# A gated scan and MLP kernel on one core: range guards of five units checked at the end, no clip of slopes, one running sum over three parts

## The chip, the cores and the metric

The kernel runs on one core of a Trainium2 chip. The metric is the device time of one execution in microseconds. Three timed executions of the kernel before took 581.10, 581.84 and 581.97 us, median 581.84 us. The engines named here are TensorE (PE, with its weight loads as PEld), VectorE (DVE), ScalarE (ACT), GpSimd (POOL) and SyncE (SP, which here only issues DMAs).

## The reference

A complex decay is applied to a state per head, step by step, and its output goes through a two-layer MLP with a quadratic-linear activation.

```
# q, k, v, a_re, a_im: [4, 8, 768, 48] f32; a_re and a_im are drawn 8 times as large
mag = sqrt(a_re**2 + a_im**2)
scale = minimum(mag, 0.999) / (mag + 1e-6)
ar, ai = a_re * scale, a_im * scale
for t in range(768):                       # S_re, S_im: [4, 8, 48, 48]
    S_re, S_im = ar*S_re - ai*S_im + k[t] (x) v[t], ar*S_im + ai*S_re
    y[t] = q[t] . S_re
x = y as 3072 rows of 384
h = x @ w_in                               # 384 -> 2048
g = where(h >= 1, h, where(h <= -1, 0, (h + 1)**2 / 4))
out = g @ w_out                            # 2048 -> 384
```

## The kernel before

**Units and blocks.** The 4 x 768 tokens are 12 units of 256 tokens: three parts of each of four sequences, in the order of `BATCH` and `PART`. Two units make a block of 512 tokens, so there are six blocks. A unit passes through `gates(u)`, which turns the step-by-step decay into closed form, and `attend(u)`, which computes its attention on PE. `moe(blk)` then runs the MLP of a block: 16 steps, each of 9 matmuls of 512 columns into `h` (line 1128) and 9 into `o` (line 1203), with ACT and DVE computing `g` and its split in two parts between them.

**What `gates` does.** `AI` holds the real part A and the imaginary part I of the decay, 128 x 768 values each (three parts `j` of 256 tokens). A Relu of A whose sum goes to a guard table `fsum` (a READ_ACCUMULATOR follows each such instruction), Ln and Exp of A for its reciprocal, the product I/A on DVE (the slope, line 589), a clip of the slope to +-1.5 (line 592), Square of the slope, a second Square with a sum of fourth powers for the guard, Ln, a combination on DVE (601), Exp, and a second combination (611) give the log decay. All these ACT instructions are recorded under one line, 576. Then come the running sum of the log decay over time, Exp of it both ways, the product with k and q (690), Arctan of the slope, a running sum of the angles, its reduction by whole turns, two Sins, and two products (799). The results `x` and `kq` are spread by DMA into the head layout `hd`, from which `attend` reads.

Units 0 and 1 hold tokens on partitions, and their running sums are matmuls with a triangle of ones on PE (630). In units 2 to 11 each running sum is three scans of 256 elements on DVE, one for each part j (lines 671 and 721), which start from the last column of the part before. The scans of the decay use min with a cap of 40.

**What else competes.** 16 weight tiles are decoded (`weights`): a load (`raw_i`, `raw_o`), three to four DVE operations of 128 x 768 (lines 440, 449, 458, 469), a cast on ACT (464), for the first five of them two matmul groups on PE (478, 479). They share DVE and ACT with the gates. In the last block `ranges(k)` loads all 16 weight tiles once more (`chk`) and runs two accumulating ACT instructions on each (lines 513, 521). Both bear on whether the fast path's assumptions hold: at the end all guard sums are compared with bounds, a flag is formed on PE and DVE, and only if one fails does `scan_all`, a slow path, run.

**What sets the order.** Every operation is noted in a `Plan` with a cost, its inputs and outputs, and for some PE work and DMAs a due time. `Plan.order` passes due times backwards, then simulates the engines and always takes the ready operation that is due first; an operation without a due time comes when nothing else is ready, unless a more urgent one is about to be (`HOLD`). The program is emitted in that order, and each engine executes its own instructions strictly in it. `Plan.emit` also fills gaps that the plan expects on PE with idle matmuls (line 1256) to keep its clock up. `tl(turn_of("g", 4), ...)` hands out four buffers in turn to `AI`, `X` and `KQ` of the units and, after them, to `chk`; a load into one waits until all who used it before are done. `ranges` also waits for the last block's inputs and for the outputs of the earlier blocks (`after=`). ACT loads a function table before each group of Ln/Exp or of Arctan/Sin (`table`); Abs, Relu, Square and Copy need none.

Of the kernel before, what the change touches and what calls it, by code (L numbers as in the profile page):

```python
# [10 lines left out]
F32 = mybir.dt.float32  # L11
F32R = mybir.dt.float32r
U32 = mybir.dt.uint32
I32 = mybir.dt.int32
AF = mybir.ActivationFunctionType
ALU = mybir.AluOpType
AX = mybir.AxisListType

P = 128
# [8 lines left out]
NJ = DM // P  # L28
NF = DFF // P
CH = 128  # L30
HC = CH // 2
U = 256
# [8 lines left out]
PLACE = [b * NPART + p for b, p in zip(BATCH, PART)]  # L41
# [3 lines left out]
SLOT = {h: i for i, h in enumerate(sum(GROUPS, ()))}  # L45

SUM = 1.0e6
RATIO = 1.5
FOURTH = 1.142**4
TINY = 1e-18  # L50
DECAY = 40.0
T_MIN = 2.0**-15 * (1.0 + 2.0**-8)
# [8 lines left out]
DMA_FIX, DMA_END, DMA_ISSUE, LANES = 2400, 50, 470, 8  # L61
LOAD, MOVE = 410.0, 240.0
# [13 lines left out]
LEAD = 9000  # L76
WARM = 0.75
ABS_ACT = 5
LO_PE = 5
INFLATE = 1.6  # L80
SPLIT_DUE = 3000
# [203 lines left out]
def dve(n, two=False):  # L285
    return 66 + n / (1.92 if two else 0.96)


def act(n, ptr=False, acc=False, psum=False):
    return (80 if psum else 100) + (92 if ptr else 0) + (92 if acc else 0) + n * (0.77 if psum else 0.84)  # L290
# [25 lines left out]
def gated_scan_moe(  # L316
    ctx: ExitStack, tc: tile.TileContext, kq, ari, art, v, wl, qn, kn, arn, ain, vn, out
):
    nc = tc.nc

    const = ctx.enter_context(tc.tile_pool(name="const", bufs=1))
# [22 lines left out]
    held = [const.tile([P, 4, CH], F32, name=f"am{g}") for g in range(2)]  # L344
    for t in held:
        nc.gpsimd.memset(t, 0.0)
    consts = [math.log(1e-6), math.pi / 2, 0.5, TINY, T_MIN, 0.0, 1.0, DECAY]
    cst = const.tile([P, len(consts)], F32, name="cst")
    for i, c in enumerate(consts):
        nc.gpsimd.memset(cst[:, i : i + 1], c)  # L350
    c_eps, c_pi2, c_half, c_tiny, c_tin, zero, c_one, c_top = (
        cst[:, i : i + 1] for i in range(len(consts))
    )
    ones = c_one
# [4 lines left out]
    minus = const.tile([P, P], F32R, name="minus")  # L359
    nc.scalar.mul(minus, ident, -1.0)  # L360
    fsum = const.tile([P, 2, NU], F32, name="fsum")
    wsum = const.tile([P, 2, NF], F32, name="wsum")
    fdec = const.tile([P, NB, NJ], F32, name="fdec")
    state = const.tile([P, 2, 2, NJ], F32, name="state")

    pl = Plan()
# [14 lines left out]
    def tl(slot, shape, dtype, name, space=None):  # L381
        if slot in banks:
            return pl.tile(slot, lambda: view(banks[slot], shape))
        return pl.tile(
            slot, lambda: (space or sb).tile(shape, dtype, tag=slot, name=name, bufs=1)
        )
# [12 lines left out]
    def turn_of(tag, n):  # L399
        k = seen.get(tag, 0)  # L400
        seen[tag] = k + 1
        return f"{tag}{k % n}"

    V_, A_, PE_ = nc.vector, nc.scalar, nc.tensor
# [126 lines left out]

    heads, vt = {}, {}
    moved = []

    def gates(u):
# [32 lines left out]
        def ac(out, src, f, r, w, tab=False, **kw):  # L570
            acc_ = kw.get("accum_out")
            cost = act(N, ptr=not isinstance(kw.get("bias", 0.0), float), acc=acc_ is not None)
            pl.op(
                "ACT",
                cost,
                lambda: A_.activation(out(), src(), f, **kw),  # L576
                r=[*r] + ([TAB] if tab else []),
                w=w,
            )

        def ve(cost, fn, r, w):
            return pl.op("DVE", cost, fn, r=r, w=w)

        ac(A, A, AF.Relu, [a], [a], accum_out=acc(0))
        if u > 1:
            table("natural_log_exp_and_others")
        ac(X0, A, AF.Ln, [a], [x0], True, bias=c_tiny)
        ac(A, X0, AF.Exp, [x0], [a], True, scale=-1.0)
        ve(dve(N), lambda: V_.tensor_tensor(I(), I(), A(), op=ALU.mult), [a], [i])
        ve(  # L590
            dve(N, True),
            lambda: V_.tensor_scalar(I(), I(), RATIO, -RATIO, op0=ALU.min, op1=ALU.max),
            [],
            [i],
        )
        ac(A, I, AF.Square, [i], [a])
        ac(X1, A, AF.Square, [a], [x1], accum_out=acc(1))
        ac(A, A, AF.Ln, [], [a], True, bias=c_one)
        ve(
            dve(N),  # L600
# [4 lines left out]
            [x0],  # L605
        )
        ac(X1, X0, AF.Exp, [x0], [x1], True, bias=c_eps)
        SUMS, sums_ = (A, a) if by_token else (X0, x0)
        ve(
            dve(N),  # L610
            lambda: V_.scalar_tensor_tensor(
                SUMS(), X0(), -math.log(0.999), X1(), op0=ALU.max, op1=ALU.add
            ),
            [x0, x1],
            [sums_],
        )
        js = ((0, 2), (2, 3))

        def running(src, part_, slots, name):
# [21 lines left out]
                out.append(R)  # L641
            return out

        if by_token:
            D_ = running(A, a, ("o0", "o1"), "dec")
            for (j0, j1), R in zip(js, D_):
                ve(
                    80,
                    lambda j0=j0, j1=j1, R=R: V_.tensor_copy(
                        state[:, b % 2, 0, j0:j1], R.get()[:, :, U - 1]  # L650
                    ),
                    [R],
                    [(STATE[0], j0)],
                )
            for e, sign in ((1, -1.0), (0, 1.0)):
                for (j0, j1), R in zip(js, D_):
                    pl.op(
                        "ACT",
                        act((j1 - j0) * U, psum=True),
                        lambda j0=j0, j1=j1, R=R, e=e, sign=sign: A_.activation(  # L660
                            X.get()[:, j0:j1, e], R.get(), AF.Exp, scale=sign
                        ),
                        r=[R, TAB],
                        w=[(X, e)],
                    )
        else:
            for j in range(NJ):
                prev = state[:, b % 2, 0, j : j + 1] if part else 0.0
                i_ = ve(
                    100 + U / 0.48,  # L670
                    lambda j=j, prev=prev: V_.tensor_tensor_scan(
                        X0()[:, j],
                        X0()[:, j],
                        c_top.to_broadcast([P, U]),
                        prev,
                        op0=ALU.add,
                        op1=ALU.min,
                    ),
                    [STATE[0]] if part else [],
                    [x0],  # L680
                )
                if j:
                    pl.loose.add(i_)
            dst = fdec[:, b] if last else state[:, b % 2, 0]
            ve(80, lambda: V_.tensor_copy(dst, X0()[:, :, U - 1]), [x0], [STATE[0]])
            ac(X1, X0, AF.Exp, [x0], [x1], True, scale=-1.0)
            ac(X0, X0, AF.Exp, [], [x0], True)

        dma(2 * size, lambda: KQ.get(), lambda: kq[place], w=[KQ], after=moved if u == 2 else ())
        ve(dve(2 * N), lambda: V_.tensor_tensor(KQ.get(), KQ.get(), X.get(), op=ALU.mult), [X], [KQ])  # L690
# [6 lines left out]
        if by_token:  # L697
            for (j0, j1), R in zip(js, running(I, i, TOKEN[u], "turns")):
                ints = lambda j0=j0, j1=j1: I()[:, j0:j1].bitcast(I32)
                ve(  # L700
                    dve((j1 - j0) * U),
                    lambda ints=ints, R=R: V_.tensor_scalar(
                        ints(), R.get(), c, None, op0=ALU.mult
                    ),
                    [R],
                    [i],
                )
                ve(
                    dve((j1 - j0) * U),
                    lambda ints=ints, R=R, j0=j0, j1=j1: V_.scalar_tensor_tensor(  # L710
                        A()[:, j0:j1], R.get(), c, ints(), op0=ALU.mult, op1=ALU.subtract
                    ),
                    [R, i],
                    [a],
                )
        else:
            for j in range(NJ):
                prev = state[:, b % 2, 1, j : j + 1] if part else 0.0
                i_ = ve(
                    100 + U / 0.48,  # L720
                    lambda j=j, prev=prev: V_.tensor_tensor_scan(
                        A()[:, j],
                        I()[:, j],
                        zero.to_broadcast([P, U]),
                        prev,
                        op0=ALU.add,
                        op1=ALU.add,
                    ),
                    [i] + ([STATE[1]] if part else []),
                    [a],  # L730
                )
                if j:
                    pl.loose.add(i_)
            ve(
                dve(N, True),
                lambda: V_.tensor_scalar(I().bitcast(I32), A(), c, None, op0=ALU.mult),
                [a],
                [i],
            )
            ve(  # L740
                dve(N),
                lambda: V_.scalar_tensor_tensor(
                    A(), A(), c, I().bitcast(I32), op0=ALU.mult, op1=ALU.subtract
                ),
                [i],
                [a],
            )
# [529 lines left out]
    for blk in range(NBLK):  # L1277
        for u in BLOCKS[blk]:
            if u > 2:
                list(gates(u))  # L1280
            if u > 1:
                attend(u)
        if blk == NBLK - 1:
            for k in range(NF):
                ranges(k)
        moe(blk)
# [264 lines left out]
```

## Time and profile before

| what | value |
| --- | --- |
| median of three timed executions | 581.84 us |
| the profiled execution's own time | 582.15 us |
| its span, first to last instruction | 580.4 us |
| mean granted PE clock | 0.988 |
| busy PE / PEld / DVE / ACT | 559.4 / 465.1 / 443.1 / 388.3 us |
| first MLP matmul starts | 75.64 us |
| last MLP matmuls end | 572.99 us |

The profiled execution took 1.75 us more than its span, which lies before the first and after the last instruction. Busy time counts idle matmuls too (24.1 us in the group of line 1256), so the 96% of PE does not mean that the whole span is useful work. "idle before <-releaser" in a line is the time for which the engine stood still before that instruction, and what ended it. An ACT or DVE instruction may start a little before the end of the one ahead of it, so what one costs on a full engine is the distance from its start to the next start.

### The profile page before, as it was taken

The page shows a single profiled execution, that of the slowest core. Times are in us where ns is not written, and L with a number is a line of the kernel's source. Part 1 is how long each engine was busy: PE and PEld are TensorE (multiplying, and loading weights), DVE is VectorE, ACT ScalarE, POOL GpSimd, SP SyncE. Part 2 cuts the span into 40 slices and gives each one's busy share as a digit, 9 for nine tenths or more (in the row PEclk, how much of TensorE's full clock was granted, in tenths as well). Part 3 has the DMA queues.
Part 4 walks back from the last instruction along what each step waited for, and adds up shares of the span by engine and source line. Part 5 has one row for each costly group of instructions (what it writes and reads, how often), then busy time and mean ns, then how long its engine had stood idle before and what let it go on. Part 6 is the DMA issues. An engine that isn't in the chain of part 4 may idle for free.

```text
span 580.4 us, 10668 instructions
## 1 busy us (share of the span) xinstructions
PE 559.4 (96%) x4250; PEld 465.1 (80%) x4250; DVE 443.1 (76%) x641; ACT 388.3 (67%) x626; POOL 3.3 (1%) x24
## 2 busy tenths in 40 slices
PE   7899789999999999999999999999999999999994
PEld 6778768888888888888888888888888888888883
DVE  6898899989979979888996787896864545454443
ACT  8886779988986766677757556667433333369972
POOL 2000000000000000000000000000000000000000
PEclk9799899999999999999999999999999999999998
DMA  8838363574460531623502513402412200087721
GB/s 348 319 115 249 135 187 148 153 238 153 152 200 19 158 110 30 215 76 97 171 1 77 190 55 101 165 3 59 152 55 84 75 1 8 13 306 256 262 88 60
DMA packets 22953, 76.66 MB, mean 132 GB/s; under 512 B 4464, under 2 KB 10224, under 8 KB 22896
## 3 DMA queue, kind: packets, MB, share of 16 engines
q1 hardware_dynamic: 22896, 75.91, 39.4%
q8 instruction: 35, 0.57, 0.4%
q14 instruction: 22, 0.18, 0.1%
HBM read 51.12 MB, written 4.72 MB: 96 GB/s over the span
## 4 chain that ended last, share of the span: by engine, by line
PE 86%; DVE 5%; DMA 3%; ACT 2%; issue 1%; SPq 1%; DVEq 0%; ACTq 0%
PE o L1203 34%; PE h L1128 34%; PE at L955 5%; PE at L999 3%; PE at L1007 3%; PE at L924 3%; PE at L895 2%; DMA hd<-kq 1%; DMA raw_i<-in_wl_dram 1%; ACT ai L576 1%; SPq L411 1%; PE o L630 1%; ACT x L576 1%; DVE kq L799 1%; DVE x L799 1%
## 5 line engine op out<-in xcount | busy, mean ns | idle before, releaser
L1128 PE MATMUL h<-xH,wi 128*128 128x512 f32 x576 | 180.9, 395 | 1.0 <-ACT xH L1098 0.8
L1203 PE MATMUL o<-gh,wo 128*128 128x512 f32 x576 | 180.0, 394 | 0.0
L1128 PEld LDWEIGHTS h<-xH,wi 128*128 128x128 f32 x576 | 105.8, 188 | 23.9 <-ACT xH L1098 1.0
L1203 PEld LDWEIGHTS o<-gh,wo 128*128 128x128 f32 x576 | 106.4, 188 | 22.3 <-issue 0.3
L1128 PE MATMUL h<-xL,wi 128*128 128x512 f32 x288 | 112.6, 391 | 0.2 <-DVE xL L1105 0.2
L1203 PE MATMUL o<-gl,wo 128*128 128x512 f32 x288 | 112.3, 390 | 0.0
L1172 DVE TENSOR_TENSOR g<-h,s 128x512 f32<-128x512 f32 x96 | 65.9, 686 | 56.2 <-ACT s L1153 48.9
L1186 ACT CAST gh<-g 128x512 fp32r<-128x512 f32 x96 | 59.3, 617 | 55.8 <-DVE g L1180 52.1
L1153 ACT ACTIVATE s<-h,cst 128x512 f32<-128x512 f32 x96 | 65.5, 684 | 42.5 <-PE h L1128 37.7
L1190 DVE TENSOR_TENSOR gl<-g,gh 128x512 fp32r<-128x512 f32 x96 | 66.0, 687 | 32.6 <-ACT gh L1186 32.3
L1128 PEld LDWEIGHTS h<-xL,wi 128*128 128x128 f32 x288 | 54.1, 188 | 12.2 <-DVE xL L1105 0.6
L1203 PEld LDWEIGHTS o<-gl,wo 128*128 128x128 f32 x288 | 54.1, 188 | 11.5
L576 ACT ACTIVATE ai<-ai 128x768 f32<-128x768 f32 x53 | 44.5, 844 | 25.6 <-DMA ai<-in_ari_dram 7.9
L1180 DVE SCALAR_TENSOR_TENSOR g<-s,g 128x512 f32<-128x512 f32 x80 | 55.3, 691 | 2.3
L955 PEld LDWEIGHTS at<-hd 96*64 96x64 f32 x704 | 32.6, 137 | 9.9 <-issue 8.2
L955 PE MATMUL at<-hd 96*64 96x128 f32 (+1 forms) x704 | 37.1, 251 | 1.8 <-DMA hd<-kq 1.8
L967 DVE COPY_PREDICATED am<-tri,at 128x512 f32<-128x512 uint32 x44 | 31.6, 738 | 2.5 <-PE at L955 2.4
L1007 PE MATMUL at<-am,V 128*64 128x128 f32 x352 | 32.9, 273 | 0.0
L999 PE MATMUL at<-hd,st 96*64 96x128 f32 x304 | 30.5, 278 | 0.0
L420 ACT ACT_TABLE_LOAD x21 | 26.9, 1283 | 0.3
L1256 PE MATMUL idle<-tri,ident 128*128 128x128 f32 x170 | 24.1, 301 | 1.8 <-POOL tri masks.py:66 1.8
L1256 PEld LDWEIGHTS idle<-tri,ident 128*128 128x128 f32 x170 | 23.2, 215 | 2.6 <-POOL tri masks.py:66 1.8
(119 smaller groups left out, 653.3 us busy)
## 6 DMA issues: line engine op xcount, KB each, us to landing
chk<-in_wl_dram SPq DMA_DIRECT2D x16, 768.0 KB, 6.5
kq<-in_kq_dram SPq DMA_DIRECT2D x12, 768.0 KB, 5.7
ai<-in_ari_dram SPq DMA_DIRECT2D x10, 768.0 KB, 6.9
V<-in_v_dram SPq DMA_DIRECT2D x12, 576.0 KB, 4.1
hd<-x SPq DMA_DIRECT2D x24, 288.0 KB, 3.5
hd<-kq SPq DMA_DIRECT2D x24, 288.0 KB, 4.1
raw_i<-in_wl_dram SPq DMA_DIRECT2D x8, 768.0 KB, 8.3
raw_o<-in_wl_dram SPq DMA_DIRECT2D x8, 768.0 KB, 4.5
```

Of the source, the lines that this page charges most:

```text
L576: lambda: A_.activation(out(), src(), f, **kw),
L955: PE_.matmul(SC.get()[o : o + HC, i + e, HC * k :], t[:, 0, ks], t[:, 1, qs], start=True, stop=True,)
L999: PE_.matmul(o_, st.get().rearrange("p h e -> p (h e)")[:, lo : lo + 64], head(h)[:, 1, cs], start=True, stop=False,)
L1007: PE_.matmul(o_, V.get()[:, c, lo : lo + 64], ams[pr // 2].get()[:, 2 * (pr % 2) + e, :], start=st is None, stop=True,)
L1128: PE_.matmul(H.get(), weight["i", f // 2].get()[:, f % 2, part, sl], x.get()[:, j, :], start=j == 0 and n == 0, stop=j == NJ - 1 and n == 2,)
L1153: lambda: A_.activation(SS.get(), H.get(), AF.Relu, bias=c_half, scale=-0.5 if spare else 0.5),
L1172: lambda: V_.tensor_tensor(G.get(), H.get(), SS.get(), op=ALU.max),
L1180: lambda: V_.scalar_tensor_tensor(G.get(), SS.get(), 1.0, G.get(), op0=ALU.min, op1=ALU.mult),
L1186: pl.op("ACT", act(T), lambda: A_.copy(GH.get(), G.get()), r=[G], w=[GH])
L1190: lambda: V_.tensor_tensor(GL.get(), G.get(), GH.get().bitcast(F32), op=ALU.subtract),
L1203: PE_.matmul(PO[m].get(), weight["o", f // 2].get()[:, f % 2, part, sl], g.get(), start=f == 0 and n == 0, stop=f == NF - 1 and n == 2,)
L1256: PE_.matmul(idle["h1"], ident, mask, start=True, stop=True)
```

## The change

Five things change in `gates`, and one function is new.

1. For units 0 to 4 (`LATE = 5`) the Relu with its sum and the second Square with its sum are left out of `gates`. The values that follow do not use their outputs as long as A is not negative.
2. For all 12 units the clip of the slope is left out.
3. For units 2 to 11 the three scans of each running sum become one scan of 768 elements (`total`). A row `again` of unsigned bytes, 0 at each part's first token and 1 elsewhere, multiplies the running value, which resets it. In parts after a sequence's first, the state of the part before is added to the first column of each part by a DVE operation of its own. The cap of 40 in the scan goes; the bound on the last value is still compared at the end.
4. The log decay is written to A instead of X0 in units 2 to 11, and the two Exps read it there.
5. `slopes(u)` reloads `AI` of units 0 to 4 and checks them: two accumulating Relus and one accumulating Abs on ACT, one DVE operation between, in which 1.142 A - |I| is formed. It is noted in the plan ahead of `ranges`, with no due time and no `after=`.

```diff
@@ -11,6 +11,7 @@
 F32 = mybir.dt.float32
 F32R = mybir.dt.float32r
 U32 = mybir.dt.uint32
+U8 = mybir.dt.uint8
 I32 = mybir.dt.int32
 AF = mybir.ActivationFunctionType
 ALU = mybir.AluOpType
@@ -45,8 +46,8 @@
 SLOT = {h: i for i, h in enumerate(sum(GROUPS, ()))}
 
 SUM = 1.0e6
-RATIO = 1.5
-FOURTH = 1.142**4
+SLOPE = 1.142
+FOURTH = SLOPE**4
 TINY = 1e-18
 DECAY = 40.0
 T_MIN = 2.0**-15 * (1.0 + 2.0**-8)
@@ -76,6 +77,7 @@
 LEAD = 9000
 WARM = 0.75
 ABS_ACT = 5
+LATE = 5
 LO_PE = 5
 INFLATE = 1.6
 SPLIT_DUE = 3000
@@ -344,11 +346,11 @@
     held = [const.tile([P, 4, CH], F32, name=f"am{g}") for g in range(2)]
     for t in held:
         nc.gpsimd.memset(t, 0.0)
-    consts = [math.log(1e-6), math.pi / 2, 0.5, TINY, T_MIN, 0.0, 1.0, DECAY]
+    consts = [math.log(1e-6), math.pi / 2, 0.5, TINY, T_MIN, 1.0]
     cst = const.tile([P, len(consts)], F32, name="cst")
     for i, c in enumerate(consts):
         nc.gpsimd.memset(cst[:, i : i + 1], c)
-    c_eps, c_pi2, c_half, c_tiny, c_tin, zero, c_one, c_top = (
+    c_eps, c_pi2, c_half, c_tiny, c_tin, c_one = (
         cst[:, i : i + 1] for i in range(len(consts))
     )
     ones = c_one
@@ -359,7 +361,12 @@
     minus = const.tile([P, P], F32R, name="minus")
     nc.scalar.mul(minus, ident, -1.0)
     fsum = const.tile([P, 2, NU], F32, name="fsum")
-    wsum = const.tile([P, 2, NF], F32, name="wsum")
+    nc.gpsimd.memset(fsum[:, 1, :LATE], 0.0)
+    wsum = const.tile([P, 2, NF + LATE], F32, name="wsum")
+    again = const.tile([P, NJ * U], U8, name="again")
+    nc.gpsimd.memset(again, 1.0)
+    for j in range(NJ):
+        nc.gpsimd.memset(again[:, j * U : j * U + 1], 0.0)
     fdec = const.tile([P, NB, NJ], F32, name="fdec")
     state = const.tile([P, 2, 2, NJ], F32, name="state")
 
@@ -530,6 +537,47 @@
         )
 
 
+
+    def slopes(u):
+        AI = tl(turn_of("g", 4), [P, 2, NJ, U], F32, f"far_{u}")
+        A, I = (lambda: AI.get()[:, 0]), (lambda: AI.get()[:, 1])
+        N = NJ * U
+        pl.op(
+            "SP",
+            DMA_ISSUE,
+            lambda: nc.sync.dma_start(AI.get(), ari[PLACE[u]]),
+            w=[AI],
+            dma=2 * P * N * 4 / LOAD,
+        )
+        pl.op(
+            "ACT",
+            act(N, acc=True),
+            lambda: A_.activation(I(), I(), AF.Abs, accum_out=wsum[:, 0, NF + u : NF + u + 1]),
+            w=[(AI, 1)],
+        )
+        pl.op(
+            "DVE",
+            dve(N),
+            lambda: V_.scalar_tensor_tensor(
+                I(), A(), SLOPE, I(), op0=ALU.mult, op1=ALU.subtract
+            ),
+            r=[(AI, 0)],
+            w=[(AI, 1)],
+        )
+        pl.op(
+            "ACT",
+            act(N, acc=True),
+            lambda: A_.activation(A(), A(), AF.Relu, accum_out=fsum[:, 0, u : u + 1]),
+            w=[(AI, 0)],
+        )
+        pl.op(
+            "ACT",
+            act(N, acc=True),
+            lambda: A_.activation(
+                I(), I(), AF.Relu, scale=-1.0, accum_out=wsum[:, 1, NF + u : NF + u + 1]
+            ),
+            w=[(AI, 1)],
+        )
 
     heads, vt = {}, {}
     moved = []
@@ -581,20 +629,16 @@
         def ve(cost, fn, r, w):
             return pl.op("DVE", cost, fn, r=r, w=w)
 
-        ac(A, A, AF.Relu, [a], [a], accum_out=acc(0))
+        if u >= LATE:
+            ac(A, A, AF.Relu, [a], [a], accum_out=acc(0))
         if u > 1:
             table("natural_log_exp_and_others")
         ac(X0, A, AF.Ln, [a], [x0], True, bias=c_tiny)
         ac(A, X0, AF.Exp, [x0], [a], True, scale=-1.0)
         ve(dve(N), lambda: V_.tensor_tensor(I(), I(), A(), op=ALU.mult), [a], [i])
-        ve(
-            dve(N, True),
-            lambda: V_.tensor_scalar(I(), I(), RATIO, -RATIO, op0=ALU.min, op1=ALU.max),
-            [],
-            [i],
-        )
         ac(A, I, AF.Square, [i], [a])
-        ac(X1, A, AF.Square, [a], [x1], accum_out=acc(1))
+        if u >= LATE:
+            ac(X1, A, AF.Square, [a], [x1], accum_out=acc(1))
         ac(A, A, AF.Ln, [], [a], True, bias=c_one)
         ve(
             dve(N),
@@ -605,14 +649,13 @@
             [x0],
         )
         ac(X1, X0, AF.Exp, [x0], [x1], True, bias=c_eps)
-        SUMS, sums_ = (A, a) if by_token else (X0, x0)
         ve(
             dve(N),
             lambda: V_.scalar_tensor_tensor(
-                SUMS(), X0(), -math.log(0.999), X1(), op0=ALU.max, op1=ALU.add
+                A(), X0(), -math.log(0.999), X1(), op0=ALU.max, op1=ALU.add
             ),
             [x0, x1],
-            [sums_],
+            [a],
         )
         js = ((0, 2), (2, 3))
 
@@ -641,6 +684,30 @@
                 out.append(R)
             return out
 
+        def total(dst, src, q, own, w):
+            if part:
+                ve(
+                    80,
+                    lambda: V_.tensor_tensor(
+                        src()[:, :, 0], src()[:, :, 0], state[:, b % 2, q], op=ALU.add
+                    ),
+                    [STATE[q]],
+                    [own],
+                )
+            ve(
+                100 + N / 0.48,
+                lambda: V_.tensor_tensor_scan(
+                    dst().rearrange("p j t -> p (j t)"),
+                    again,
+                    src().rearrange("p j t -> p (j t)"),
+                    0.0,
+                    op0=ALU.mult,
+                    op1=ALU.add,
+                ),
+                [own] if own is not w else [],
+                [w],
+            )
+
         if by_token:
             D_ = running(A, a, ("o0", "o1"), "dec")
             for (j0, j1), R in zip(js, D_):
@@ -664,27 +731,11 @@
                         w=[(X, e)],
                     )
         else:
-            for j in range(NJ):
-                prev = state[:, b % 2, 0, j : j + 1] if part else 0.0
-                i_ = ve(
-                    100 + U / 0.48,
-                    lambda j=j, prev=prev: V_.tensor_tensor_scan(
-                        X0()[:, j],
-                        X0()[:, j],
-                        c_top.to_broadcast([P, U]),
-                        prev,
-                        op0=ALU.add,
-                        op1=ALU.min,
-                    ),
-                    [STATE[0]] if part else [],
-                    [x0],
-                )
-                if j:
-                    pl.loose.add(i_)
+            total(A, A, 0, a, a)
             dst = fdec[:, b] if last else state[:, b % 2, 0]
-            ve(80, lambda: V_.tensor_copy(dst, X0()[:, :, U - 1]), [x0], [STATE[0]])
-            ac(X1, X0, AF.Exp, [x0], [x1], True, scale=-1.0)
-            ac(X0, X0, AF.Exp, [], [x0], True)
+            ve(80, lambda: V_.tensor_copy(dst, A()[:, :, U - 1]), [a], [STATE[0]])
+            ac(X1, A, AF.Exp, [a], [x1], True, scale=-1.0)
+            ac(X0, A, AF.Exp, [a], [x0], True)
 
         dma(2 * size, lambda: KQ.get(), lambda: kq[place], w=[KQ], after=moved if u == 2 else ())
         ve(dve(2 * N), lambda: V_.tensor_tensor(KQ.get(), KQ.get(), X.get(), op=ALU.mult), [X], [KQ])
@@ -714,23 +765,7 @@
                     [a],
                 )
         else:
-            for j in range(NJ):
-                prev = state[:, b % 2, 1, j : j + 1] if part else 0.0
-                i_ = ve(
-                    100 + U / 0.48,
-                    lambda j=j, prev=prev: V_.tensor_tensor_scan(
-                        A()[:, j],
-                        I()[:, j],
-                        zero.to_broadcast([P, U]),
-                        prev,
-                        op0=ALU.add,
-                        op1=ALU.add,
-                    ),
-                    [i] + ([STATE[1]] if part else []),
-                    [a],
-                )
-                if j:
-                    pl.loose.add(i_)
+            total(A, I, 1, i, a)
             ve(
                 dve(N, True),
                 lambda: V_.tensor_scalar(I().bitcast(I32), A(), c, None, op0=ALU.mult),
@@ -1281,6 +1316,8 @@
             if u > 1:
                 attend(u)
         if blk == NBLK - 1:
+            for u in range(LATE):
+                slopes(u)
             for k in range(NF):
                 ranges(k)
         moe(blk)
```

## The prediction

> **What bounds the kernel now.** I read the page's 40 slices first, then the busy time by stretch, and then, since the answer pointed to the first 85 us, the timelines of ACT, DVE and PE there.
>
> From the page, the busy tenths of PE and ACT:
>
> ```profile
> PE   7899789999999999999999999999999999999994
> ACT  8886779988986766677757556667433333369972
> ```
>
> From the busy time by stretch (columns: length; busy us of PE, PEld, DVE, ACT, POOL; granted clock; DMA share; GB/s):
>
> ```profile
> 0.00:16.00 16.00, 10.56 (x60) 9.29 (x60) 10.98 (x17) 13.15 (x21) 3.28 (x24) 0.93 0.88 355
> 16.00:45.00 29.00, 27.43 (x144) 21.66 (x146) 26.95 (x37) 23.65 (x38) 0.00 (x0) 0.92 0.58 199
> 45.00:61.00 16.00, 12.66 (x239) 11.72 (x238) 13.84 (x20) 10.74 (x18) 0.00 (x0) 1.00 0.89 292
> 61.00:76.00 15.00, 13.73 (x194) 13.01 (x194) 14.10 (x18) 10.90 (x18) 0.00 (x0) 0.89 0.25 78
> 76.00:85.00 9.00, 7.00 (x51) 5.03 (x50) 7.78 (x13) 8.31 (x15) 0.00 (x0) 1.00 0.60 168
> 85.00:260.00 175.00, 174.88 (x1400) 144.92 (x1399) 156.88 (x225) 136.62 (x212) 0.00 (x0) 1.00 0.43 140
> 260.00:425.00 165.00, 165.00 (x1292) 137.27 (x1289) 137.44 (x198) 104.71 (x161) 0.00 (x0) 1.00 0.31 96
> 425.00:510.00 85.00, 85.00 (x605) 70.35 (x604) 40.78 (x62) 30.07 (x52) 0.00 (x0) 1.00 0.15 44
> 510.00:567.00 57.00, 57.00 (x253) 47.18 (x252) 30.25 (x44) 46.78 (x94) 0.00 (x0) 1.00 0.63 226
> ```
>
> From 85 us to the last MLP matmul PE is busy without a break (174.88 of 175, 165 of 165, 85 of 85, 57 of 57) at full clock. The change takes no matmul away. So behind 85 us nothing taken from ACT or DVE is worth time, and the end moves by as much as the start of that unbroken stretch moves. Ahead of it PE is only filled with idle matmuls; the stretch is a chain of units 0, 1 and 2 through ACT, DVE and DMA, with the weight decode as filler. That is the stage in which the change has to pay. A change of this kernel below about 0.2% (1.16 us) can't be told from none.
>
> **The change part by part: the guards of units 0 and 1.** This is ACT's timeline of the start (start, length, instruction); rows that carry no term are left out:
>
> ```profile
> 4.04 0.84 ACT L576 ACTIVATE ai<-ai 128x768 f32<-128x768 f32 x1 [2.01 <-DMA ai<-in_art_dram]
> ...
> 4.88 0.29 ACT L360 ACTIVATE minus<-ident 128x128 fp32r<-128x128 f32 x1
> 5.08 0.93 ACT L576 ACTIVATE x<-ai,cst 128x768 f32<-128x768 f32 x1
> 5.94 0.84 ACT L576 ACTIVATE ai<-ai 128x768 f32<-128x768 f32 x1
> ...
> 6.78 0.83 ACT L576 ACTIVATE ai<-x 128x768 f32<-128x768 f32 x1
> ...
> 9.22 0.84 ACT L576 ACTIVATE ai<-ai 128x768 f32<-128x768 f32 x1
> 10.10 0.84 ACT L576 ACTIVATE x<-ai 128x768 f32<-128x768 f32 x1
> ...
> 10.94 0.83 ACT L576 ACTIVATE ai<-ai 128x768 f32<-128x768 f32 x1
> ...
> 12.50 0.83 ACT L576 ACTIVATE x<-ai 128x768 f32<-128x768 f32 x1
> ...
> 13.46 0.94 ACT L576 ACTIVATE ai<-ai,cst 128x768 f32<-128x768 f32 x1
> 14.30 0.92 ACT L576 ACTIVATE x<-x,cst 128x768 f32<-128x768 f32 x1
> ...
> 16.75 0.83 ACT L576 ACTIVATE ai<-ai 128x768 f32<-128x768 f32 x1
> ...
> 19.50 0.60 ACT L660 ACTIVATE x<-o 128x512 f32<-128x512 f32 x1 [1.47 <-PE o L630]
> ...
> 25.00 1.28 ACT L420 ACT_TABLE_LOAD   x1
> ```
>
> ACT stands still until unit 0's A lands, and then no row has a wait in brackets until 19.50: for 13 us ACT is the limit. Four of these instructions go: the Relus of units 0 (4.04) and 1 (5.94), each with its read of the sum, and their second Squares (10.10 and 12.50). On a full engine each costs the distance to the next start: 4.04 to 4.88, 5.94 to 6.78 and 10.10 to 10.94 are 0.84 us each, 12.50 to 13.46 is 0.96. That is 3.48 us, 3.36 if I count the last like the others. I take 3.4.
>
> Does something else take ACT's place? DVE's rows and the first running sums on PE:
>
> ```profile
> 7.64 0.96 DVE L589 TENSOR_TENSOR ai<-ai 128x768 f32<-128x768 f32 x1 [3.52 <-ACT ai L576]
> 8.63 0.56 DVE L592 TENSOR_SCALAR ai<-ai 128x768 f32<-128x768 f32 x1
> 15.47 0.95 DVE L611 SCALAR_TENSOR_TENSOR ai<-x 128x768 f32<-128x768 f32 x1
> 16.57 4.15 PE L630 MATMUL o<-tri,ai 128*128 128x256 f32 x12
> 21.41 2.12 PE L630 MATMUL o<-tri,ai 128*128 128x256 f32 x12
> ```
>
> DVE waits 3.52 us for ACT, so it is not late at first. Unit 0's chain alone, without any queue: the first Exp would start one Relu earlier at 5.94, the product at 6.8, Square at 7.8, Ln at 8.6, the combination at 9.5, Exp at 10.5, the second combination at 11.4, against 15.47 now. So latency alone would allow 4.1 us; ACT's load, with unit 1 between, gives 3.4. The landing of I of unit 0 is not told by any row before the product at 7.64; were it there only then, the chain from the product on still starts a clip and two ACT instructions shorter, 2.2 us (0.56 + 2 x 0.84). So the step is worth 2.2 to 4.1 us, and I keep 3.4.
>
> **The clip.** On DVE 0.56 us each. In units 0 and 1 it lies beside a busy ACT: Square of unit 0 starts at 9.22, when ACT has just finished other work. I cost it at nothing; ACT's queue hides it, and if ACT has a hole there it is up to 0.56 more gain. In unit 2 it is part of DVE's load before the MLP, 0.56. In units 3 to 11 PE's unbroken stretch hides it.
>
> **Unit 2.** Its Relu (16.75) stands ahead of a wait of 1.47 us for PE, so its going is worth nothing. Its second Square stands in a stretch where ACT is busy 10.74 of 16 us: nothing. The scans:
>
> ```profile
> 95.39 2.03 DVE L721 TENSOR_TENSOR_SCAN ai<-ai,state,cst 128x256 f32<-128x256 f32 x3
> 54.71 0.17 DVE L685 COPY state<-x 128x3 f32<-128x3 f32 x1
> ```
>
> Three scans in a row take 2.03 us. One over 768 elements takes no more than that if it costs the same for each element, and no less than an elementwise operation on 768 (0.96); whether a row of bytes as a multiplier slows it no row shows, so a loss cannot be excluded: at twice the time, 2 more us for each scan. I take it nearest to the scans, 2.0, and the added addition at the 0.17 of the copy of three columns, so two running sums cost 0.3 more at most. [...] Against the 0.56 of the clip, unit 2 comes out within 0.3 us of zero, and I count zero. The addition waits for the state, as the scans did; behind it on DVE nothing new waits. The second running sum writes A, which the two Exps now read, but a table load and Arctan stand between already. The memsets of `again` come last on POOL, which is done at about 4 us; the first scan is at 50.
>
> **The checks at the end.** Five loads of 768 KB, fifteen accumulating ACT instructions at 0.84 (12.6 us) and five DVE ones at 0.96 (4.8 us). The rows that decide where they can lie:
>
> ```profile
> 424.06 1.75 DVE L799 TENSOR_TENSOR kq<-kq,ai 128x1536 f32<-128x1536 f32 x1
> 450.51 1.22 SPq L411 DMA_DIRECT2D hd<-kq  x2
> 510.82 39.23 SPq L425 DMA_DIRECT2D chk<-in_wl_dram  x16
> 561.83 0.19 ACT L521 ACTIVATION_READ_ACCUMULATOR chk<-chk,cst 128x1 f32 x1
> 566.86 6.13 PE o L1203 x27
> ```
>
> Counting `turn_of("g", 4)` through the units, the first `slopes` takes the buffer of unit 10's KQ, the next three those of unit 11's AI, X and KQ, the fifth the first's again. Those are free after the last product (425.8) or the last spreads (about 455), and `slopes` waits for nothing else, while `chk` begins only at 510.82. ACT is idle 54.9 of the 85 us from 425 to 510 and DVE 44.2, so 12.6 and 4.8 fit, and DMA is busy 0.15. Cost nothing. Behind a `slopes` instruction that waits for its load stand the activations of the MLP on ACT, behind its load on SP the moves of `xr`: both wait only if the load is later than planned, and PE is three steps ahead of `o`. If that cover is gone, the third rival has the price.
>
> **The sum.** 582.15 - 3.4 = 578.75 us for the profiled execution, which lay 0.31 above the median; against the median, 578.4 us.
>
> **The rivals.** *First: DVE takes over.* From 16 to 76 us DVE is busy 54.89 of 60 us. If the units come 3.4 us earlier while the weight decode, which filled ACT's delays, does not shrink, DVE has 56.6 us for that; the plan may put decode back in front of the units. For it speaks the density, against it that DVE waited in the first 8 us. Then only DVE's own saving is left, 0.56 of unit 2's clip: 581.3 us. That the guards go without moving anything comes to the same.
>
> *Second: the clock.* The first twelve sums took 4.15 us, the next twelve 2.12. If the earlier sums come while the clock is still up, another 2.0 us go: 576.4 us. [...]
>
> *Third, and slower: ACT overflows at the end.* If `slopes` stands among the `chk` work and not before it, ACT, 46.78 of 57 us busy, gets 12.6 more. The last check ends at 562.0 now; with MLP work in a third of the time the rest lasts 12.6 / 0.67 = 18.8 us, to 580.8, against PE's end at 573.0. Less the 3.4 gained, 4.4 late: 586.2 us. It decides once `slopes` runs later than about 495. Against it speak the buffers.
>
> *Fourth, slower: DVE waits for a weight.* These rows show it today on a small scale:
>
> ```profile
> 52.27 6.91 DMA raw_i<-in_wl_dram
> 59.19 0.56 DVE L440 TENSOR_SCALAR y_i<-raw_i 128x768 uint32<-128x768 uint32 x1 [0.74 <-DMA raw_i<-in_wl_dram]
> 61.44 0.86 PE L895 MATMUL o<-ident,hd 96*128 96x96 f32 x4 [3.12 <-DVE am L967]
> ```
>
> DVE waits for a load of 6.91 us in a stretch with DMA at 0.89, and the copies that attention needs stand behind it; PE stands still for 3.12 us. If an earlier unit chain makes DVE come to the decode at the load's issue, the wait is 6.9 instead of 0.74: 6.2 lost less 3.4 gained, 584.6 us. It decides when the wait there passes 4.1 us (0.74 + 3.4).
>
> **How the numbers follow.** The forecast 0.52: the row by row saving on a full engine. First rival 0.22, half of it within 0.2% of no change. Second 0.10. Third 0.04, fourth 0.12, either of them at times small enough to end near no change (0.02). Faster by over 0.2%: 0.52 + 0.10 + 0.11 = 0.73; within 0.13; slower 0.14. The predicted time is the likeliest, 578.4. The range reaches from 575.7, the second rival with unit 0's chain at 4.1 instead of 3.4, to 582.2, which takes in the first rival and leaves out most of the slower ones.
>
> **What would show it.** Right: ACT's rows from 4 to about 14 us without a hole, the second combination of unit 0 at about 12 us, the first table of Arctan at about 21.6 instead of 25.0, the first MLP matmul at about 72.2 instead of 75.64, PE without a break from then on, and the last `slopes` before 510. The clock rival: twelve sums in about 2.1 us. Wrong: a table load early but the first MLP matmul at its old place (first rival); a long bracket with `raw` ahead of line 967 or PE idle behind it (fourth); checks that end past PE (third); a scan of 768 elements over 2.1 us; PE idle anywhere behind 85 us.

## The result and the profile after

Twenty executions of the changed kernel took 579.89 us in the median (576.22 to 582.30), twenty of the kernel before 581.85. One of the twenty before took 831.70 us, in a slow state, and is left out of the ratio. The means of the others are 579.35 and 582.47 us; the ratio is 0.9947 with a 95% interval of 0.9926 to 0.9967: 0.53% faster, or 3.1 us of 581.85 (1.9 to 4.3). The two medians are only 2.0 us apart. Both kernels scatter, the changed one over 6.1 us and the one before over 5.5. The profiled execution of the changed kernel took 580.46 us, with a span of 578.7, 1.7 less than before.

In the new line numbers the ACT instructions of the gates are 624, the slope 638, the two combinations 645 and 654, the running sums on PE 673, decode 447, 456, 465 and 476, the MLP matmuls 1163 and 1238, and the late checks 548 to 576. Busy time by stretch in the kernel after, with the stretches and columns of before (two stretches are left out):

```profile
0.00:16.00 16.00, 11.11 (x65) 10.59 (x66) 9.73 (x14) 10.35 (x12) 4.08 (x27) 0.89 0.90 359
16.00:45.00 29.00, 27.19 (x173) 21.71 (x171) 26.30 (x35) 22.09 (x34) 0.00 (x0) 0.94 0.64 217
45.00:61.00 16.00, 15.59 (x287) 14.02 (x288) 15.24 (x21) 11.70 (x19) 0.00 (x0) 1.00 0.85 279
61.00:76.00 15.00, 12.41 (x116) 10.80 (x117) 13.37 (x20) 10.89 (x17) 0.00 (x0) 0.89 0.33 95
85.00:260.00 175.00, 174.18 (x1391) 144.06 (x1389) 157.25 (x208) 136.20 (x207) 0.00 (x0) 1.00 0.41 130
425.00:510.00 85.00, 84.58 (x597) 69.52 (x597) 44.61 (x67) 41.36 (x79) 0.00 (x0) 1.00 0.26 82
510.00:567.00 57.00, 57.00 (x251) 46.60 (x250) 30.32 (x45) 46.78 (x93) 0.00 (x0) 1.00 0.60 220
```

ACT falls from 13.15 to 10.35 us in the first 16, so it is no longer full there. PE is no longer without a break behind 85 us: 174.18 of 175, 84.58 of 85. The start, and some later rows to which the text comes back, from ACT's timeline, DVE's and PE's (rows in between are left out):

```profile
4.01 0.93 ACT L624 ACTIVATE x<-ai,cst 128x768 f32<-128x768 f32 x1 [1.67 <-POOL kT L360]
7.96 0.84 ACT L624 ACTIVATE ai<-ai 128x768 f32<-128x768 f32 x1 [0.23 <-DVE ai L638]
10.60 0.94 ACT L624 ACTIVATE ai<-ai,cst 128x768 f32<-128x768 f32 x1
16.73 1.88 ACT L727 ACTIVATE x<-o 128x512 f32<-128x512 f32 x4 [3.24 <-DVE state L716]
22.49 1.28 ACT L427 ACT_TABLE_LOAD   x1
```

```profile
6.97 1.83 DVE L638 TENSOR_TENSOR ai<-ai 128x768 f32<-128x768 f32 x2 [2.86 <-DMA ai<-in_art_dram]
9.87 0.96 DVE L645 SCALAR_TENSOR_TENSOR x<-ai,x 128x768 f32<-128x768 f32 x1 [1.07 <-ACT ai L624]
10.74 0.56 DVE L447 TENSOR_SCALAR y_i<-raw_i 128x768 uint32<-128x768 uint32 x1
11.57 0.96 DVE L645 SCALAR_TENSOR_TENSOR x<-ai,x 128x768 f32<-128x768 f32 x1 [0.27 <-ACT ai L624]
12.45 0.95 DVE L654 SCALAR_TENSOR_TENSOR ai<-x 128x768 f32<-128x768 f32 x1
52.04 1.76 DVE L699 TENSOR_TENSOR_SCAN ai<-again,ai 128x768 f32<-128x768 uint8 x1
116.55 0.56 DVE L447 TENSOR_SCALAR y_i<-raw_i 128x768 uint32<-128x768 uint32 x1 [2.65 <-DMA raw_i<-in_wl_dram]
```

```profile
13.54 4.18 PE L673 MATMUL o<-tri,ai 128*128 128x256 f32 x12 [3.14 <-DVE ai L654]
60.87 1.20 PE L930 MATMUL o<-ident,hd 96*128 96x96 f32 x8
70.74 1.22 PE L1163 MATMUL h<-xH,wi 128*128 128x512 f32 x2 [2.49 <-ACT xH L1133]
78.53 0.73 PE L1163 MATMUL h<-xH,wi 128*128 128x512 f32 x2 [1.85 <-DVE g L1207]
122.92 0.73 PE L1163 MATMUL h<-xH,wi 128*128 128x512 f32 x2 [0.54 <-DVE g L1207]
421.06 0.50 PE L1238 MATMUL o<-gl,wo 128*128 128x512 f32 x1 [0.33 <-DVE gl L1225]
435.39 0.73 PE L1163 MATMUL h<-xH,wi 128*128 128x512 f32 x2 [0.29 <-DVE g L1207]
```

The first sums start 3.0 us earlier (13.54 against 16.57), the Arctan table 2.5 (22.49 against 25.00), the first MLP matmul 4.9 (70.74 against 75.64). Yet the span is only 1.7 shorter. To see where the lead goes I gave every matmul of MLP and attention its usual distance to the next, added these up along each trace, and compared the times at which the same sum is reached. The table gives the lead over the kernel before in us, so more is earlier:

| time in the kernel before, us | after | e1 guards only | e9 three scans | e11 decode held | e5 no late checks | e6 checks at 490 |
| --- | --- | --- | --- | --- | --- | --- |
| 47.7 | 2.1 | -0.8 | 4.4 | 0.9 | 3.4 | 2.1 |
| 76.6 | 4.8 | 1.7 | 6.9 | 2.9 | 5.9 | 4.9 |
| 88.0 | 4.6 | 2.4 | 5.0 | 3.0 | 3.7 | 4.5 |
| 123.1 | 4.6 | 2.4 | 5.0 | 3.0 | 3.7 | 4.5 |
| 144.1 | 3.3 | 1.4 | 4.5 | 3.2 | 3.7 | 4.7 |
| 413.3 | 3.7 | 1.1 | 4.0 | 3.0 | 3.7 | 5.2 |
| 454.7 | 2.4 | 0.2 | 2.8 | 2.6 | 3.7 | 5.2 |
| 570.1 | 1.8 | 0.2 | 2.8 | 2.6 | 3.7 | 4.9 |

The lead does not come from the start of units 0 and 1 alone. Between the first two rows of the table, by the same count, it goes from 1.8 us at 55.4 to 5.0 at 61.4. There PE waited 3.12 us in the kernel before, for the copy of line 967 that stands behind a decode (the prediction shows the row, at 61.44); in the kernel after, PE comes to the same matmuls at 60.87 without a wait. Behind the MLP's first steps the column "after" loses 1.3 us between 123 and 144, behind a decode that waited 2.65 us for its load, 1.35 between 413 and 455, where the late checks run, and 0.5 more near 517, where the weight checks run; the cause of that last loss stays open.

### The profile page after: what moved, and what is told of

Read it like the earlier page. It is cut to its first block, busy times and chain, and to the rows that moved or that the text cites. A ratio compares the mean times of both kernels' runs of the same rounds, so it can differ in the third digit from the quotient of the medians.

```text
span 578.7 us, 10631 instructions
## 1 busy us (share of the span) xinstructions
PE 558.2 (96%) x4240; PEld 463.1 (80%) x4240; DVE 439.1 (76%) x610; ACT 391.7 (68%) x636; POOL 4.1 (1%) x27
## 4 chain that ended last, share of the span: by engine, by line
PE 70%; DVE 12%; DMA 7%; ACT 5%; issue 2%; SPq 2%; DVEq 0%; ACTq 0%
PE h L1163 27%; PE o L1238 26%; PE at L990 5%; PE at L1042 3%; PE at L1034 3%; DMA far<-in_ari_dram 2%; PE at L959 2%; SPq L418 2%; PE at L930 2%; ACT ai L624 2%; DMA hd<-kq 1%; DMA raw_i<-in_wl_dram 1%; DVE g L1207 1%; DMA kq<-in_kq_dram 1%; PE o L673 1%
## 5 line engine op out<-in xcount | busy, mean ns | idle before, releaser
L1238 PEld LDWEIGHTS o<-gh,wo 128*128 128x128 f32 x576 | 106.2, 188 | 22.5 <-ACT gh L1221 0.4
L624 ACT ACTIVATE ai<-ai 128x768 f32<-128x768 f32 x48 | 40.3, 844 | 18.0 <-DMA ai<-in_ari_dram 6.6
L699 DVE TENSOR_TENSOR_SCAN ai<-again,ai 128x768 f32<-128x768 uint8 x20 | 35.1, 1753 | 0.3
L741 DVE TENSOR_TENSOR kq<-kq,x 128x1536 f32<-128x1536 f32 x12 | 21.1, 1754 | 6.8 <-DMA kq<-in_kq_dram 4.2
```

What stands on the lines that cost most here:

```text
L699: lambda: V_.tensor_tensor_scan(dst().rearrange("p j t -> p (j t)"), again, src().rearrange("p j t -> p (j t)"), 0.0, op0=ALU.mult, op1=AL ...
L1238: PE_.matmul(PO[m].get(), weight["o", f // 2].get()[:, f % 2, part, sl], g.get(), start=f == 0 and n == 0, stop=f == NF - 1 and n == 2,)
```

## The experiments

Theory at the start: ScalarE's load by the guards of units 0 and 1 sets the start; clip and scan are worth nothing. Rivals: clip or scan pay; the new order pays; late checks cost something. All ratios below are to the kernel before, with 95% intervals.

**e1, the guards alone moved.** In the kernel after, clip and three scans are back (main lines of the edit, shortened):

```diff
+            lambda: V_.tensor_scalar(I(), I(), RATIO, -RATIO, op0=ALU.min, op1=ALU.max),
...
-            total(A, A, 0, a, a)
+            for j in range(NJ):
...
```

> The kernel after with the clip and the three scans of before put back: only the guards of units 0 to 4 are moved. Theory (the guards on a full ScalarE pay): first MLP matmul 3 to 5 us earlier than in the kernel before, whole time 1.5 to 3.5 us below it. Rival (the clip and the single scan pay): first MLP matmul within 1 us of before, time within 1.2 us of before.

Ratio 1.0005 (0.9984 to 1.0025): no gain, against the theory. The first sums start only 0.8 us early, the first MLP matmul (73.77) 1.9. DVE's and PE's timelines of e1 (638 is the clip here, 648 and 658 the combinations, 462 decode):

```profile
8.70 1.02 DVE L638 TENSOR_SCALAR ai<-ai 128x768 f32<-128x768 f32 x2
12.10 1.82 DVE L648 SCALAR_TENSOR_TENSOR x<-ai,x 128x768 f32<-128x768 f32 x2
13.84 0.95 DVE L462 SCALAR_TENSOR_TENSOR raw_i<-raw_i 128x768 uint32<-128x768 uint32 x1
14.71 1.82 DVE L658 SCALAR_TENSOR_TENSOR ai<-x 128x768 f32<-128x768 f32 x2
```

```profile
15.81 3.97 PE L677 MATMUL o<-tri,ai 128*128 128x256 f32 x12 [5.41 <-DVE ai L658]
```

Two things hold the chain where ACT did: the clips, ahead of the Squares, and a weight decode, of which the plan puts two instructions (10.63 and 11.23) ahead of the first combinations and one (13.84) ahead of the second.

**e2, the clip alone gone; e3, the single scan alone; e10, both, with all guards in place.**

```diff
...
-            lambda: V_.tensor_scalar(I(), I(), RATIO, -RATIO, op0=ALU.min, op1=ALU.max),
...
```

```diff
-            for j in range(NJ):
...
+            total(A, A, 0, a, a)
```

> The kernel before without the clip of slopes, nothing else changed. Theory: within 0.6 us of before (the clip lies beside a busy ScalarE in units 0 and 1). Rival (clip pays): 1.5 us or more below before.

> The kernel before with one scan of 768 over a reset row, nothing else changed. Theory: a scan of about 1.75 us instead of 2.03, an addition of 0.16 in two parts of three, within 0.6 us of before. Rival (scan pays): 1.5 us or more below before.

> The kernel before without the clip and with the single scan, all guards in place. Theory: first sums at about 16.5 us as in before, because ScalarE still has the guards, and no gain in time, within 1.5 us of before or slower. Rival (clip and scan together carry the gain): first sums before 15 us, time 2 us or more below before.

e2: 1.0011 (0.9988 to 1.0034). e3: 1.0045 (1.0018 to 1.0071), slower. e10: 1.0032 (1.0015 to 1.0050), slower. The first sums start at 16.70, 16.58 and 16.52 us, as before: with the guards in place neither edit moves them. Without the guards moved the other two edits give no gain, as the theory says; but e3, expected within 0.6 us of before, is 2.6 us slower by its ratio. In the profile of e3, PE loses time early in the MLP; one of the waits, from DVE's and PE's timelines:

```profile
99.52 1.75 DVE L702 TENSOR_TENSOR kq<-kq,x 128x1536 f32<-128x1536 f32 x1
101.37 1.76 DVE L660 TENSOR_TENSOR_SCAN ai<-again,ai 128x768 f32<-128x768 uint8 x1
103.05 0.70 DVE L963 COPY_PREDICATED am<-tri,at 128x512 f32<-128x512 uint32 x1
```

```profile
103.80 0.44 PE L995 MATMUL at<-hd,st 96*64 96x128 f32 x4 [1.65 <-DVE am L963]
```

A copy that attention needs stands behind a scan of 1.76 us that can no longer be interrupted between its parts. Whether that or the rest of the new order makes e3 slower, no run separates.

**e4, four instructions left out, the order of before kept.** The plan counts them, but they are not issued; their guard sums are zero, so the range of A and the slope is not checked for units 0 and 1.

```diff
-                lambda: A_.activation(out(), src(), f, **kw),
+                (lambda: None) if skip else lambda: A_.activation(out(), src(), f, **kw),
```

> The kernel before with its order of instructions unchanged, but the first Relu and the second Square of units 0 and 1 are not issued (their guard sums are set to zero, so the range of A and the slope is not checked there). Theory (ScalarE's load alone sets the start): first running sums on TensorE about 3.4 us earlier, first MLP matmul 2 to 3.4 us earlier than before, time 2 to 3.4 us below before. Rival (it is the new order that pays): first sums earlier, but the first MLP matmul within 1 us of before.

Ratio 0.9983 (0.9956 to 1.0009), first sums at 16.39, the first MLP matmul at 74.98, 0.7 us early. DVE's timeline of e4:

```profile
10.62 0.56 DVE L441 TENSOR_SCALAR y_i<-raw_i 128x768 uint32<-128x768 uint32 x1 [0.69 <-DMA raw_i<-in_wl_dram]
13.08 0.95 DVE L602 SCALAR_TENSOR_TENSOR x<-ai,x 128x768 f32<-128x768 f32 x1
```

The theory falls here. ACT is free now, but DVE waits for the first weight to land, decodes it in three instructions, and only then comes to the combination, as the old order says. In the kernel before the same rows stand on DVE, and none of its rows from 8.63 to 18.08 has a wait either:

```profile
10.81 0.55 DVE L440 TENSOR_SCALAR y_i<-raw_i 128x768 uint32<-128x768 uint32 x1
11.40 0.96 DVE L449 SCALAR_TENSOR_TENSOR raw_i<-raw_i,y_i 128x768 uint32<-128x768 uint32 x1
12.39 0.96 DVE L458 SCALAR_TENSOR_TENSOR raw_i<-raw_i 128x768 uint32<-128x768 uint32 x1
13.26 0.95 DVE L601 SCALAR_TENSOR_TENSOR x<-ai,x 128x768 f32<-128x768 f32 x1
```

Its combination starts at 13.26 there and at 13.08 in e4. ACT looked like the only limit, but the two engines ended together.

**e11, the guards moved as in e1, and no decode before both second combinations.**

```diff
             r=[RAW],
             w=[Y],
+            after=combos[:2],
```

> The kernel with the guards alone moved (clip and three scans in place), but no weight is decoded on VectorE before both second combinations of units 0 and 1. Theory (decode that stands ahead on VectorE eats what the guards free): first sums at 14.0 to 14.8 us instead of 15.8. Rival (the clip's own 0.56 us in each chain is all that holds them): first sums within 0.4 us of 15.8.

First sums, from PE's timeline of e11:

```profile
14.76 3.47 PE L680 MATMUL o<-tri,ai 128*128 128x256 f32 x11 [3.62 <-DVE ai L660]
```

1.05 of the 2.27 us between e1 (15.81) and after (13.54) were the decode; the remaining 1.2 most likely go with the clips, which are still there. The time is 0.9993 (0.9977 to 1.0009), not told apart from e1.

**e9, the kernel after with three scans again.** The edit is e3's, reversed.

> The kernel after with the three scans of before put back; guards moved and clip gone as in after. Theory (guards and clip together free the start, the scan adds nothing): first sums at about 13.5 us, first MLP matmul within 1 us of after's 70.7, time within 1.5 us of after. Rival (all three parts are needed): first MLP matmul at 73 us or later, time at least 2 us above after.

First sums at 13.53, first MLP matmul at 68.74. The start needs guards and clip, not the scan. The time does not follow so clearly: the ratio, 0.9982 (0.9965 to 1.0000), is a gain of 1.0 us where after has 3.1, with intervals that just touch. The medians (580.61 against 579.89) are 0.7 us apart, and in the profile of e9 PE's MLP ends 1.0 us earlier than in that of after. So what the single scan is worth in the new order stays open, and with it how much of the 0.53% is the start's. The first MLP matmul is even earlier than in after for another reason, told under the clock below.

**e5, no late checks (units 0 to 4 are not checked at all); e6, checks from 490 us; e7, checks from 510 us.**

```diff
-            for u in range(LATE):
-                slopes(u)
```

```diff
-            dma=2 * P * N * 4 / LOAD,
+            dma=2 * P * N * 4 / LOAD, after=handover[NBLK - 1],
```

```diff
-            dma=2 * P * N * 4 / LOAD,
+            dma=2 * P * N * 4 / LOAD, after=[*handover[NBLK - 1], *finals],
```

> The kernel after without the reload and check of units 0 to 4 at the end (their ranges are not checked at all); the order is the same up to about 410 us. Theory A (the late checks delay TensorE in block 4): the lead over before stays at about 3.7 us from 145 us to the end instead of falling to 2.4 at 450, so 1.2 to 1.6 us faster than after. Theory B (late checks are hidden, the loss there is the plan's): within 0.4 us of after.

> The kernel after with the late checks held back until the last block's inputs are in place (about 490 us). Theory A: no loss of lead between 410 and 450, 0.8 to 1.6 us faster than after, if ScalarE's idle time from 490 to 516 takes the 12.6 us. Third rival of the prediction: the weight checks are pushed past TensorE's end, 1 to 4 us slower than after.

> The kernel after with the late checks held back as the weight checks are (about 510 us). Third rival of the prediction: ScalarE overflows, the last check ends at about 580 us, time about 4 to 8 us above after. Theory: no loss between 410 and 450 but ScalarE has only 10 us free from 510 to 567, so the end comes 2 to 8 us late.

e5: 0.9934 (0.9910 to 0.9958). e6: 0.9942 (0.9922 to 0.9962). e7: 1.0060 (1.0030 to 1.0090). From 410 to 440 us, first after, then e6:

```profile
410.00:440.00 30.00, 29.26 (x232) 23.55 (x231) 20.34 (x26) 16.97 (x35) 0.00 (x0) 1.00 0.41 144
```

```profile
410.00:440.00 30.00, 30.00 (x261) 24.80 (x260) 19.28 (x25) 10.21 (x18) 0.00 (x0) 1.00 0.13 47
```

With the late checks out of this stretch PE has no gap, and neither e5 nor e6 loses lead there (table), where after and e9 lose 1.35 and 1.1. The loss depends on the order: by the same count e1 loses 0.9, e8 (below) 0.8, e11 only 0.35. The profiles show theory A; the times of e5 and e6 point the same way, by 0.13% and 0.05%, well inside their intervals. In e7 the checks end behind PE's last MLP matmuls (which end at 572.2):

```profile
577.73 0.19 ACT L528 ACTIVATION_READ_ACCUMULATOR chk<-chk,cst 128x1 f32 x1
```

```profile
578.42 0.19 PE L1344 MATMUL at<-ok,cst 128*1 128x4 f32 x2 [6.22 <-DVE ok L1340]
```

That is the prediction's third rival, at its price: 0.6% of 582.5 is 3.5 us slower than before, against 4.4 forecast. By the profiles the five units can be checked between 490 and 510 at a loss of 0.3 us of lead (e6: 5.2 to 4.9), and not 20 us later.

**e8, LATE = 2.**

```diff
-LATE = 5
+LATE = 2
```

> The kernel after with LATE = 2: only the guards of units 0 and 1 are moved to the end, those of units 2 to 4 stay in place. Theory: first MLP matmul within 1 us of that of after, since only units 0 and 1 lie on the path; fewer late checks cost less, so 0 to 1.5 us faster than after. Rival (units 2 to 4 matter): first MLP matmul 1 us or more later, time 1 us or more above after.

Ratio 0.9955 (0.9931 to 0.9979), first MLP matmul at 70.12. Leaving the guards of units 2 to 4 in place costs nothing that shows; they are not on the path. A gain over after from the fewer late checks does not show either.

**e12, e6 with idle matmuls in the whole of each planned gap.**

```diff
-WARM = 0.75
+WARM = 1.0
```

> The kernel with the late checks at 490 us, and idle matmuls in all of each planned gap on TensorE instead of three quarters. Theory (the half clock over the first MLP matmuls costs about 1.3 us): granted clock 1.00 from 66 to 85 us, lead over before at 90 us about 5.5 instead of 4.5, 1 us faster than the run without it. Rival: idle matmuls get in the way, the same or up to 1.5 us slower.

Ratio 0.9935 (0.9910 to 0.9961), not to be told from e6. Around the first MLP matmuls the clock stayed down: from 71 to 76 us the granted clock is 0.68 here and 0.69 in after. The expectation of a clock of 1.00 failed, so what the half clock there (0.50 from 71 to 73 us in after) costs was not measured. The lead at 88 us was 5.7 against 4.5 in e6; it comes from the first sums, which took 2.20 us instead of e6's 4.18:

```profile
13.49 2.20 PE L673 MATMUL o<-tri,ai 128*128 128x256 f32 x12 [0.77 <-DVE ai L654]
```

Ahead of them 78 idle matmuls ran instead of 58, and PE stood still for 0.77 us instead of 3.14 in after. That may be why; but in e9 the sums took 2.20 us behind a wait of 3.50 (see below), so one execution does not tell.

## Why the prediction was right, and which steps were not

**The stage was right, the sum in part by luck.** 3.4 us were forecast, 3.1 (1.9 to 4.3) measured, and the lead begins in units 0 and 1. The first sums, 3.4 us earlier by the forecast (13.2), came at 13.5, the Arctan table, forecast at 21.6, at 22.5. But the forecast carries one saving unchanged to the end, and the profile shows something else: a lead of 3.0 us at the first sums, 2.1 at 47.7, 4.8 at 76.6, 1.8 at the end. The wait of 3.12 us ahead of the matmuls at 61.44, which the prediction counted only as a danger (its fourth rival), is gone, and the first MLP matmul came at 70.7 instead of the forecast 72.2; this gain is not in the sum. The losses behind 123 us are not in it either. That the measured total lies near 3.4 is luck to that extent. Whether earlier units or the new order ended that wait no run separates: in e4, with the order of before, 2.46 us of it are left, in e1 1.07.

**"The clip: I cost it at nothing" failed.** The guards were credited with all 3.4 us; alone they give 0.8 at the first sums (e1), or 0.2 in the old order (e4), the clip alone nothing (e2), guards and clip together 3.0 (after, e9). ACT was full and DVE's chain ended together with it, so each edit alone only uncovers the other. The step before it, "does something else take ACT's place?", asked the right thing, but looked only at unit 0's own chain without any queue; the decode that stands ahead of the combinations on DVE was in the trace of before (rows 10.81 to 12.39). The first rival, that DVE takes over, is what happens to e1 and e4; in the whole change the clips are gone from DVE, and the first combination comes ahead of decode (9.87 against 10.74).

**The landing of I**, which no row of the prediction showed, is at 6.97 in after: the product, forecast at 6.8, waits for it (2.86 us until DMA). That is a new bound ahead of the chain. Behind it, unit 0's second combination (12.45) stands on DVE behind unit 1's first (11.57), which waits for unit 1's Ln on ACT (10.60); the forecast's chain had no unit 1 in it. Which of the two makes 3.0 of the 3.4 no run separates.

**"Cost nothing" for the late checks failed** in the profile: 1.35 us, because ACT and DVE, idle for 43% and 32% of the time from 410 to 440, still delay instructions that PE waits for (rows 421.06 and 435.39) when the checks stand ahead of them. The buffers were free no later than the prediction said, and the checks ran from 416 to 465.

**"PE without a break from then on" failed.** Besides the late checks, after lost 1.3 us at 123 to 144; e6, with the same order up to 410, lost nothing there. The same decode in e6 waited less for its load (after: 2.65 us):

```profile
115.05 0.56 DVE L447 TENSOR_SCALAR y_i<-raw_i 128x768 uint32<-128x768 uint32 x1 [1.09 <-DMA raw_i<-in_wl_dram]
```

e5 and e7, with the same order up to 410 too, lost nothing there either. That loss belongs to the execution, not to the change; it can be part of the scatter of 6 us.

**The scan** costs 1.76 instead of 2.03, so a little under the 2.0 taken. That unit 2 comes out near zero fits the profiles: between 47.7 and 76.6 after gains 2.7 us of lead and e9, with three scans, 2.5.

**The clock rival** is real, and it changes from execution to execution. In the kernel before the granted clock was at 0.50 and 0.57 under the first twelve sums (from 16.57) and at 1.00 under the next twelve (from 21.41):

```profile
15.00:18.00 3.00, 1.94 (x6) 1.57 (x7) 3.00 (x4) 3.00 (x6) 0.00 (x0) 0.50 1.02 418
18.00:21.00 3.00, 3.00 (x12) 2.49 (x11) 1.90 (x6) 1.27 (x4) 0.00 (x0) 0.57 1.02 416
21.00:24.00 3.00, 3.00 (x18) 2.45 (x16) 2.45 (x2) 2.81 (x7) 0.00 (x0) 1.00 0.96 311
```

Twelve first sums in e5 and e9:

```profile
13.47 3.43 PE L673 MATMUL o<-tri,ai 128*128 128x256 f32 x12 [2.28 <-DVE ai L654]
```

```profile
13.53 2.20 PE L670 MATMUL o<-tri,ai 128*128 128x256 f32 x12 [3.50 <-DVE ai L651]
```

After needs 4.18, at a granted clock of 0.50 from 13.5 to 18 us, and e5, with the same instructions up to 410, 3.43; e9's 2.20 lie near the 2.12 that the second twelve of before took at 1.00. What decides it the runs do not show. The wait ahead of the sums does not separate them: they were slow behind waits of 2.28 us (e5) and 3.14 (after), and fast behind one of 3.50 (e9). Idle matmuls that end close ahead of the sums were there only in e12 (0.77 us), and one execution leaves their part open. The price was right, 2.3 us of lead at 47.7 (e9 against after), but the forecast that it reaches the end was not: at 88 us 0.4 are left. In part that is the MLP's first wait for `g`, 2.87 us in e9 against 1.85 in after (78.53).

## What to carry to other kernels

An engine without a gap is the only bound only if nothing ends together with it: before crediting a removal, take the in-order queue of the next engine row by row, with the loads that its filler work waits for. Price edits together where two chains end within a microsecond; here neither the guards nor the clip alone showed a gain. A total that agrees does not show that its terms do: follow the lead along the trace. Work "with no due time" on half-idle engines is not free where a tightly coupled loop runs on them; look for the place where it delays least, here the last block's first 20 us, where the profile lost 0.3 us instead of 1.35.

## What was not expected of the hardware

The same twelve matmuls of the first sums took 4.18, 3.43 or 2.20 us, in after, e5 and e9. In after they ran at half the clock (0.50 from 13.5 to 18 us); over the whole execution the granted clock is 0.989 in after, 0.992 in e5 and 0.995 in e9. In after it fell again for a few us around the first MLP matmuls (0.69 from 71 to 76 us), behind a wait of 2.49 us, although idle matmuls had run until 68.25. The load ahead of the decode at 116 us made DVE wait 2.65 us in one execution and 1.09 in another with the same instructions before it; in the first PE then lost 1.3 us, in the second nothing.
